# The row of -max by DMA in a fused attention and MLP kernel, with every fifth query in a tile of the maxima

## The chip, the cores and the metric

The kernel runs on one core of a Trainium2 chip. The metric is the device time of one execution in microseconds (us), as the median of several; a separate execution is recorded by the hardware profiler and gives the profile and the trace. The engines are TensorE (PE for its products, PEld for the loads of its stationary operand), VectorE (DVE), ScalarE (ACT), GpSimd (POOL) and SyncE (SP, which here only issues DMAs).

## The reference

```python
def _attn_ref(q, k, v):                     # (2, 8, 1152, 64) each
    q_pool = q.reshape(B, H, S // 2, 2, D).mean(axis=3)
    scores = scale * np.matmul(q_pool, k.transpose(0, 1, 3, 2))
    scores = scores - np.max(scores, axis=-1, keepdims=True)
    attn = np.exp(scores)
    attn = attn / (np.sum(attn, axis=-1, keepdims=True) + 1e-09)
    return np.matmul(attn, v)

x = attn_out.transpose(0, 2, 1, 3).reshape(1152, 512)
r = np.maximum(x @ moe_w_in, 0.0);  x = (r * r) @ moe_w_out            # 512 -> 2048 -> 512
out = ((x @ moe2_w_a) * (x @ moe2_w_b)) @ moe2_w_out                   # 512 -> 1536 -> 512
```

There are 16 heads (batch times heads), each with 576 pooled queries and 1152 keys of 64 values. Every row of scores has its exact maximum taken off before the exponential.

## The kernel before

Every operand of a product is split into a high and a low part (float32r), and a product of two such operands is three products, so that accuracy stays near float32. The attention runs head by head, written out in one order for all engines; each engine works through its own list in that order.

For a head `h`, `trans_q` and `trans_k` transpose the pooled queries and the keys by TensorE and spread the parts by DMAs into the operands `qa` (high part of q, twice, 128 rows), `q0` (low part), `k1` (high and low part of k) and `kb` (high part of k, with rows of ones below). `maxima(h, n)`, n = 0 to 7, computes scores with the queries on the 116 output partitions: five tiles of 116 queries (`QO`: 0, 116, 232, 348, 460, the last two overlap) by three chunks of 384 keys, two products each, into PSUM tiles `pm`; VectorE reduces each to its negated maximum in `mh`. In such a product the slice of `qa` or `q0` is the stationary operand and `k1` the moving one. `max_split` takes the minimum over the three chunks (`nm`) and splits it into a high and a low part in `mz`. `trans_max` turns that into two rows: five TensorE transposes of 66 rows into a PSUM tile `px`, of which ScalarE copies rows 64 and 65 into rows 64 and 65 of `qb`, the moving operand whose first 64 rows are the low part of q. With the ones in `kb` the product of `kb` and `qb` then adds the negated maximum.

`scores(h, t)`, t = 0 to 8, computes scores again with 128 keys on the partitions and 576 queries in two halves, as `k1` by `qa` plus `kb` by `qb`, into a PSUM tile `ps`; ScalarE makes the exponential `ex` and its high part `eh`, VectorE (or POOL for t = 1, 4, 7) the low part `el`. `values(h, t)` multiplies with v into `o`, two steps later. `normal` copies `o` to `os`; for each pair of heads `outputs` makes the reciprocal sums (`dn` by DMA, `rd`, and `rb` on POOL), and `outputs_end` transposes `rb` into a PSUM tile `pr`, multiplies (`xt` on VectorE), and writes the operand of the MLP, `xh` by ScalarE and `xl` by VectorE. All of `pm`, `ps`, `px`, `pr`, `pq` and `pk` share one ring of three PSUM buffers, so a tile waits for the reader of the third tile before it.

The loop interleaves two heads: in step t of head h stand `scores(h, t)`, `maxima(h + 1, t + 3)` up to t = 4 and `maxima(h + 2, t - 6)` from t = 6 on, and `values` of step t - 2. `max_split(h + 1)` stands at t = 5, `trans_max(h + 1)` at t = 6, `outputs_end` at t = 5 of odd heads from h = 3 on. From h = 7 on, at t = 4 and 8, `w_step` also prepares weights of the MLP: it loads them (`raw`) and splits them on ScalarE (`wa`, `whi`), VectorE (`wx`) and POOL (`wlo`).

Behind the attention come the two MLPs, which the change doesn't touch.

Of the kernel before, what the change touches and what calls it, by code (L numbers as in the profile page):

```python
# [9 lines left out]
F32 = mybir.dt.float32  # L10
F32R = mybir.dt.float32r
# [10 lines left out]
def kernel(  # L22
# [18 lines left out]
    nc = tc.nc  # L41
# [135 lines left out]


    TQ = 116
    QO = [0, 116, 232, 348, 460]  # L180
    NQ = len(QO)
    NCH = S // CW

    KO = [0, 2, 4, 6, 1, 3, 5, 7, 8]
# [3 lines left out]
    def attention(gs):  # L188
        with ExitStack() as es:
# [30 lines left out]
            NB = 3  # L220
            k1 = [(pp if i == (NH - 3) % NB else ap).tile([P, S], F32R, name=f"k1_{i}") for i in range(NB)]
            kb = [(pp if i == (NH - 3) % NB else ap).tile([P, S], F32R, name=f"kb_{i}") for i in range(NB)]
            qa = [(pp if i == (NH - 3) % NB else ap).tile([P, SQ], F32R, name=f"qa_{i}") for i in range(NB)]
            vv = [(pp if i == (NH - 3) % NB else ap).tile([P, KT, 2, VW], F32R, name=f"vv_{i}") for i in range(NB)]
            qb = [ap.tile([P, SQ], F32R, name=f"qb_{i}") for i in range(2)]
            q0 = [pp.tile([P, SQ], F32R, name=f"q0_{i}") for i in range(2)]
            mz = [pp.tile([TQ, NQ, D + 2], F32R, name=f"mz_{i}") for i in range(2)]

            def constant(t, x):
                nc.gpsimd.memset(t.bitcast(F32), x)  # L230
# [7 lines left out]
            first_k = k1[2].rearrange("p (t a d) -> p t a d", a=2, d=D)  # L238
            first_q = [kb[i][:QP, :QT * P].rearrange("p (t a d) -> p t a d", a=2, d=D) for i in (1, 2)]
            constant(first_q[1][:, :, 1, :], 0.0)  # L240
            constant(mz[0], 0.0)
            constant(qb[0][D:], 0.0)
            constant(q0[1][D:], 0.0)

# [2 lines left out]
            def copy(e, out, in_):  # L247
                if e == "A":
                    nc.scalar.copy(out, in_)
                else:  # L250
                    engines[e].tensor_copy(out, in_)

            def move(out, in_, queue=nc.sync):

                queue.dma_start(out=out.bitcast(F32), in_=in_.bitcast(F32))

            def less(e, out, x, hi):
                engines[e].tensor_tensor(out=out, in0=x, in1=hi.bitcast(F32), op=ALU.subtract)  # L258

            def ps_tile(name, dt=F32):  # L260
                return ps_p.tile([P, 2, 512], dt, tag="ps", name=name)

            def halves(t):
                return t.rearrange("p (b w) -> p b w", b=2)
# [55 lines left out]
            def maxima(h, n):  # L320
                if n == 0:
                    mh[h] = ap.tile([TQ, NQ * NCH], F32, tag="mh", bufs=2, name=f"mh{h}")
                ps = ps_tile(f"pm{h}_{n}")
                todo = [divmod(j, NCH) for j in range(2 * n, min(2 * n + 2, NQ * NCH))]
                for b, (i, c) in enumerate(todo):
                    qs = slice(QO[i], QO[i] + TQ)
                    ks = slice(c * CW, (c + 1) * CW)
                    nc.tensor.matmul(ps[:TQ, b, :CW], qa[h % NB][:, qs], k1[h % NB][:, ks], start=True, stop=False)  # L328
                    nc.tensor.matmul(ps[:TQ, b, :CW], q0[h % 2][:, qs], k1[h % NB][:, ks], start=False, stop=True)  # L329
                w = len(todo)  # L330
                nc.vector.tensor_reduce(  # L331
                    out=mh[h][:, 2 * n:2 * n + w], in_=ps[:TQ, :w, :CW], op=ALU.max, axis=AX.X, negate=True
                )

            def max_split(h):
                z = mz[h % 2]
                nm = ap.tile([TQ, NQ], F32, tag="nm", bufs=2, name=f"nm{h}")
                nc.vector.tensor_reduce(
                    out=nm, in_=mh.pop(h).rearrange("p (i c) -> p i c", c=NCH), op=ALU.min, axis=AX.X
                )  # L340
                nc.vector.tensor_copy(z[:, :, D], nm)
                less("V", z[:, :, D + 1], nm, z[:, :, D])

            def by_tiles(ps):

                return (slice(0, 464), ps[:, 0, :464]), (slice(464, SQ), ps[:, 1, 4:TQ])

            def trans_max(h, e="A"):
                ps = ps_tile(f"px{h}", F32R)
                for i in range(NQ):  # L350
                    nc.tensor.matmul(
                        ps[:D + 2, i // 4, (i % 4) * TQ:(i % 4 + 1) * TQ], mz[h % 2][:, i, :], idr[:TQ, :TQ],
                        is_transpose=True, start=True, stop=True,
                    )
                for sl, src in by_tiles(ps):
                    copy(e, qb[h % 2][D:D + 2, sl], src[D:D + 2].bitcast(F32))


            ex, eh, el, ou = {}, {}, {}, {}
# [1 line left out]
            def scores(h, t):  # L361
                ps = ps_tile(f"ps{h}_{t}")
                ks = slice(t * P, (t + 1) * P)
                for c in range(2):
                    sl = slice(c * CQ, (c + 1) * CQ)
                    nc.tensor.matmul(ps[:, c, :CQ], k1[h % NB][:, ks], qa[h % NB][:, sl], start=True, stop=False)  # L366
                    nc.tensor.matmul(ps[:, c, :CQ], kb[h % NB][:, ks], qb[h % 2][:, sl], start=False, stop=True)  # L367
                e = ex[h, t] = ap.tile([P, SQ], F32, tag="ex", bufs=3, name=f"ex{h}_{t}")
                nc.scalar.activation(halves(e), ps[:, :, :CQ], AF.Exp, scale=SCALE)  # L369

# [70 lines left out]
            def first_head():  # L441
                idle(NWARM)
                pool_q(0, "V")
                x = qs_t.pop(0)
                hi, lo = first_q
                nc.scalar.copy(first_k[:, :, 0], kin[0])
                nc.vector.tensor_copy(hi, x[:, :, None, :].to_broadcast([QP, QT, 2, D]))
                less("V", lo[:, :, 0], x, hi[:, :, 0])
                less("V", first_k[:, :, 1], kin.pop(0), first_k[:, :, 0])
                for src, dst, eng in ((hi, qa[0], "A"), (lo, q0[0], "V")):  # L450
                    ps = ps_tile(f"fq{eng}", F32R)
                    for t in range(QT):
                        nc.tensor.matmul(
                            ps[:, t % 2, (t // 2) * QP:(t // 2 + 1) * QP], src[:, t].rearrange("p a d -> p (a d)"),
                            idr[:QP, :QP], is_transpose=True, start=True, stop=True,
                        )
                    copy(eng, halves(dst), ps[:, :, :CQ].bitcast(F32))
                move(qb[0][:D], q0[0][:D])
                for part, n in enumerate((6, 3)):
                    ps = ps_tile(f"fk{part}", F32R)  # L460
                    for i in range(n):
                        nc.tensor.matmul(
                            ps[:, i // 3, (i % 3) * P:(i % 3 + 1) * P],
                            first_k[:, KO[6 * part + i]].rearrange("p a d -> p (a d)"), idr,
                            is_transpose=True, start=True, stop=True,
                        )
                    for b in range(n // 3):
                        c0 = (2 * part + b) * CW
                        copy("AVA"[2 * part + b], k1[0][:, c0:c0 + CW], ps[:, b, :CW].bitcast(F32))
# [8 lines left out]
            for n in range(NM):  # L478
                maxima(0, n)
                if n == 1:  # L480
                    trans_q(1)
                    constant(mz[1], 0.0)
                    constant(qb[1][D:], 0.0)
                    constants(1)
                    move(kb[0][:D], k1[0][:D])
                    load(2)
                    load(3)
            max_split(0)
            idle(7)
            trans_max(0)  # L490
            for n in range(AHEAD - 1):
                maxima(1, n)
            split_v(0)
# [8 lines left out]
            for h in range(NH + 1):  # L502
                last = h == NH - 1
                for t in range(KT if h < NH else 2):
                    if h + 1 < NH and t == NM - AHEAD:
                        max_split(h + 1)
                    if t == 0 and h + 1 < NH:
                        move(qb[(h + 1) % 2][:D], q0[(h + 1) % 2][:D])
                    if h + 2 < NH:
                        if t == 0:  # L510
                            trans_q(h + 2)
# [5 lines left out]
                        exp_hi(h, t)  # L517
                    while later:
                        later.pop(0)()
                    if h + 1 < NH:  # L520
                        if t == NM - AHEAD + 1:
                            trans_max(h + 1)
                    if h % 2 and h > 1 and t == NM - AHEAD:
                        outputs_end((h - 3) // 2, rb)
                    if h + 1 < NH and t < NM - AHEAD:
                        maxima(h + 1, t + AHEAD)
                    if h + 2 < NH and t >= KT - AHEAD:
# [15 lines left out]
                    if t == 5 and h + 2 < NH:  # L543
                        split_v(h + 2)
                        load_v(h + 4)
                    if NH - 9 <= h < NH - 1 and t in (4, 8):
                        w_step(NE)
                    if last:
# [235 lines left out]
```

## Time and profile before

| | |
|---|---|
| median of 3 runs | 767.36 us (766.59 to 767.93) |
| profiled execution | 767.84 us, span 766.1 us |
| TensorE products / loads | 741.7 us busy (97%) / 714.9 us (93%), 4629 each |
| VectorE, ScalarE, POOL | 507.6 us (66%), 409.5 us (53%), 147.5 us (19%) |
| granted TensorE clock | 0.996 of full speed on average |

The span is the time from the first to the last recorded instruction. A busy TensorE is not one at its peak: products are pipelined, and the length shown for one contains the latency of the pipeline, so their starts are closer than their lengths. How much each step costs is read from the distance between starts.

### The profile page before, as it was taken

Reading aid. Unit: us, or ns where it says so; the run is one execution under the profiler, and the core shown is the slowest. Engines: PE = TensorE matmul, PEld = TensorE weight load, DVE = VectorE, ACT = ScalarE, POOL = GpSimd, SP = SyncE. Lnnn points to the kernel's source line nnn. Section 1 sums busy time; section 2 is a strip of 40 time slices with the busy share of each in tenths; the row PEclk is TensorE's granted clock in tenths of the full one; section 3 lists DMA queues with packets and bytes.
Section 4 is the critical chain, followed back from the end, with each engine's and each line's share of the span. In section 5 each row is a group of like instructions: output and inputs, shape, how many; then the busy total and the mean of one; then the engine's idle time right before and its main releaser. Section 6 shows DMA issues by size and latency. Waiting matters only on the chain.

```text
span 766.1 us, 12264 instructions
## 1 busy us (share of the span) xinstructions
PE 741.7 (97%) x4629; PEld 714.9 (93%) x4629; DVE 507.6 (66%) x807; ACT 409.5 (53%) x716; POOL 147.5 (19%) x132
## 2 busy tenths in 40 slices
PE   8999999989999999899999999999999999999998
PEld 7899999979899898889999999999999988999986
DVE  6777878767888888556973298746687831377511
ACT  2677777767778677764642376423455522355300
POOL 5444344432454453200310000000000000000000
PEclk9999999999999999999999999999999999999999
DMA  6755555564655451100431232212333320043022
GB/s 176 211 132 141 125 130 127 128 173 114 165 141 136 126 113 38 37 9 1 137 112 56 83 111 82 83 56 83 96 126 119 128 83 29 29 136 111 1 56 68
DMA packets 57547, 76.75 MB, mean 100 GB/s; under 512 B 7248, under 2 KB 41936, under 8 KB 57488
## 3 DMA queue, kind: packets, MB, share of 16 engines
q1 hardware_dynamic: 57168, 75.38, 35.7%
q10 hardware_dynamic: 320, 0.59, 0.3%
q8 instruction: 36, 0.59, 0.3%
q14 instruction: 23, 0.19, 0.1%
HBM read 49.81 MB, written 2.36 MB: 68 GB/s over the span
## 4 chain that ended last, share of the span: by engine, by line
PE 82%; DVE 8%; ACT 3%; issue 3%; DMA 2%; SPq 1%; POOL 0%; ACTq 0%; DVEq 0%; POOLq 0%
PE o L388 11%; PE pm L328 5%; PE pm L329 4%; PE y L580 4%; PE y L581 4%; PE y L579 4%; PE ps L366 4%; PE ps L367 4%; PE a L579 3%; PE a L581 3%; PE b L581 3%; PE b L579 3%; PE a L580 3%; PE b L580 3%; PE o L581 3%; PE o L580 3%
## 5 line engine op out<-in xcount | busy, mean ns | idle before, releaser
L331 DVE TENSOR_REDUCE mh<-pm 116x2 f32<-116x768 f32 (+1 forms) x128 | 114.7, 901 | 40.0 <-PE pm L329 39.2
L388 PE MATMUL o<-eh,vv 128*66 128x288 f32 x576 | 138.8, 297 | 0.7 <-ACT os L398 0.7
L369 ACT ACTIVATE ex<-ps 128x576 f32<-128x576 f32 x144 | 93.8, 652 | 49.4 <-PE ps L367 47.1
L258 DVE TENSOR_TENSOR el<-ex,eh 128x576 fp32r<-128x576 f32 x99 | 87.1, 880 | 22.3 <-ACT eh L373 22.3
L373 ACT CAST eh<-ex 128x576 fp32r<-128x576 f32 x144 | 97.1, 674 | 4.6
L258 POOL TENSOR_TENSOR el<-ex,eh 128x576 fp32r<-128x576 f32 x45 | 66.5, 1478 | 151.6 <-ACT eh L373 87.3
L328 PE MATMUL pm<-k,qa 128*116 128x384 f32 x240 | 85.1, 355 | 4.7 <-DVE xt L424 2.6
L388 PE MATMUL o<-el,vv 128*66 128x288 f32 x288 | 85.2, 296 | 0.9 <-POOL el L258 0.6
L366 PE MATMUL ps<-qa,k 128*128 128x288 f32 x288 | 83.7, 305 | 0.1
L329 PE MATMUL pm<-k,q 128*116 128x384 f32 x240 | 82.3, 343 | 0.0
L367 PE MATMUL ps<-qb,kb 128*128 128x288 f32 x288 | 81.3, 296 | 0.0
L388 PEld LDWEIGHTS o<-eh,vv 128*66 128x66 f32 x576 | 78.5, 137 | 1.1 <-ACT os L398 0.9
L145 DVE TENSOR_TENSOR wlo<-wx,whi 128x512 fp32r<-128x512 f32 x56 | 38.5, 687 | 54.5 <-ACT whi L111 54.5
L111 ACT CAST whi<-wx 128x512 fp32r<-128x512 f32 x68 | 42.1, 619 | 51.4 <-DVE wx L130 51.4
L580 PE MATMUL y<-gl,whi 128*128 128x384 f32 x192 | 64.8, 338 | 0.6 <-DVE gl L570 0.6
L581 PE MATMUL y<-gh,wlo 128*128 128x384 f32 x192 | 64.8, 338 | 0.0
L579 PE MATMUL y<-gh,whi 128*128 128x384 f32 x192 | 64.7, 337 | 0.0
L579 PE MATMUL h<-xh,whi 128*128 128x384 f32 (+1 forms) x172 | 56.0, 325 | 0.7 <-ACT r L598 0.7
L580 PE MATMUL h<-xl,whi 128*128 128x384 f32 (+1 forms) x172 | 55.9, 325 | 0.0
L581 PE MATMUL h<-xh,wlo 128*128 128x384 f32 (+1 forms) x172 | 55.9, 325 | 0.0
L366 PEld LDWEIGHTS ps<-qa,k 128*128 128x128 f32 x288 | 54.7, 190 | 0.5 <-ACT ex L369 0.4
L367 PEld LDWEIGHTS ps<-qb,kb 128*128 128x128 f32 x288 | 54.7, 190 | 0.0
(110 smaller groups left out, 1684.0 us busy)
## 6 DMA issues: line engine op xcount, KB each, us to landing
raw<-in_moe_w_out_dram SPq DMA_DIRECT2D x28, 512.0 KB, 3.4
raw<-in_moe_w_in_dram SPq DMA_DIRECT2D x16, 512.0 KB, 3.8
raw<-in_moe_w_a_dram SPq DMA_DIRECT2D x12, 512.0 KB, 3.5
raw<-in_moe_w_b_dram SPq DMA_DIRECT2D x12, 512.0 KB, 3.5
qin<-in_q_dram SPq DMA_DIRECT2D x16, 288.0 KB, 3.5
kin<-in_k_dram SPq DMA_DIRECT2D x16, 288.0 KB, 3.7
vin<-in_v_dram SPq DMA_DIRECT2D x16, 288.0 KB, 3.2
k<-kt SPq DMA_DIRECT2D x28, 160.0 KB, 2.7
```

The costliest lines, as they stand in the source:

```text
L258: engines[e].tensor_tensor(out=out, in0=x, in1=hi.bitcast(F32), op=ALU.subtract)
L328: nc.tensor.matmul(ps[:TQ, b, :CW], qa[h % NB][:, qs], k1[h % NB][:, ks], start=True, stop=False)
L329: nc.tensor.matmul(ps[:TQ, b, :CW], q0[h % 2][:, qs], k1[h % NB][:, ks], start=False, stop=True)
L331: nc.vector.tensor_reduce(out=mh[h][:, 2 * n:2 * n + w], in_=ps[:TQ, :w, :CW], op=ALU.max, axis=AX.X, negate=True)
L366: nc.tensor.matmul(ps[:, c, :CQ], k1[h % NB][:, ks], qa[h % NB][:, sl], start=True, stop=False)
L367: nc.tensor.matmul(ps[:, c, :CQ], kb[h % NB][:, ks], qb[h % 2][:, sl], start=False, stop=True)
L369: nc.scalar.activation(halves(e), ps[:, :, :CQ], AF.Exp, scale=SCALE)
L373: nc.scalar.copy(eh[h, t], ex[h, t])
L388: nc.tensor.matmul(ou[h][:VW, c, :CQ], w, x[:, c * CQ:(c + 1) * CQ], start=t == 0 and i == 0, stop=t == KT - 1 and i == 2,)
L579: nc.tensor.matmul(ps, lh, rh, start=i == 0, stop=False)
L580: nc.tensor.matmul(ps, lh, rl, start=False, stop=False)
L581: nc.tensor.matmul(ps, ll, rh, start=False, stop=i == n - 1)
```

## The change

The maxima take their queries with a step of five: tile i of a head holds the queries i, i + 5, i + 10 and so on. `qa`, `q0` and `qb` grow from 576 to 580 columns (`SM`), the last four of which are zero, so that five tiles of 116 cover them. Then the five values that a partition p holds in `mz` are those of the queries 5p to 5p + 4, and the whole of `mz`, read partition by partition, is the row in its natural order. Two DMAs, one for the high and one for the low part, write it into rows 64 and 65 of `qb`; `trans_max`, its transposes, its PSUM tile and its copies are gone, and so are the seven dummy products ahead of the first of them. In `scores` the two products `k1` by `qa` come first, then the two `kb` by `qb`. `outputs_end` moves ahead of `max_split` and of the scores of its step. The first three loads of weights are issued in step 6 of head 5.

```diff
-    QO = [0, 116, 232, 348, 460]
-    NQ = len(QO)
+    NQ = 5
+    SM = NQ * TQ
...
-            mz = [pp.tile([TQ, NQ, D + 2], F32R, name=f"mz_{i}") for i in range(2)]
+            mz = [ap.tile([TQ, 2, NQ], F32R, name=f"mz_{i}") for i in range(2)]
...
-                    qs = slice(QO[i], QO[i] + TQ)
+                    hi, lo = (t.rearrange("p (q i) -> p i q", i=NQ)[:, i] for t in (qa[h % NB], q0[h % 2]))
                     ks = slice(c * CW, (c + 1) * CW)
-                    nc.tensor.matmul(ps[:TQ, b, :CW], qa[h % NB][:, qs], k1[h % NB][:, ks], start=True, stop=False)
-                    nc.tensor.matmul(ps[:TQ, b, :CW], q0[h % 2][:, qs], k1[h % NB][:, ks], start=False, stop=True)
+                    nc.tensor.matmul(ps[:TQ, b, :CW], hi, k1[h % NB][:, ks], start=True, stop=False)
+                    nc.tensor.matmul(ps[:TQ, b, :CW], lo, k1[h % NB][:, ks], start=False, stop=True)
...
-            def max_split(h):
+            def max_split(h, queue=nc.sync):
...
-                nc.vector.tensor_copy(z[:, :, D], nm)
-                less("V", z[:, :, D + 1], nm, z[:, :, D])
...
+                nc.vector.tensor_copy(z[:, 0], nm)
+                less("V", z[:, 1], nm, z[:, 0])
+                for a in range(2):
+                    move(qb[h % 2][D + a:D + a + 1], z[:, a], queue)
...
-                for c in range(2):
-                    sl = slice(c * CQ, (c + 1) * CQ)
-                    nc.tensor.matmul(ps[:, c, :CQ], k1[h % NB][:, ks], qa[h % NB][:, sl], start=True, stop=False)
-                    nc.tensor.matmul(ps[:, c, :CQ], kb[h % NB][:, ks], qb[h % 2][:, sl], start=False, stop=True)
+                for i, (w, x) in enumerate(((k1, qa[h % NB]), (kb, qb[h % 2]))):
+                    for c in range(2):
+                        sl = slice(c * CQ, (c + 1) * CQ)
+                        nc.tensor.matmul(ps[:, c, :CQ], w[h % NB][:, ks], x[:, sl], start=i == 0, stop=i == 1)
...
-            max_split(0)
-            idle(7)
-            trans_max(0)
+            max_split(0, nc.scalar)
...
+                    if h % 2 and h > 1 and t == NM - AHEAD:
+                        outputs_end((h - 3) // 2, rb)
                     if h + 1 < NH and t == NM - AHEAD:
                         max_split(h + 1)
...
-                    if h + 1 < NH:
-                        if t == NM - AHEAD + 1:
-                            trans_max(h + 1)
-                    if h % 2 and h > 1 and t == NM - AHEAD:
-                        outputs_end((h - 3) // 2, rb)
...
+                    if h == NH - 11 and t == 6:
+                        w_load(3)
```

Three places show what moves. The first is TensorE in steps 5 and 6 of head 3, before; `ps3_5` are the scores of head 3, step 5, `pm5_0` the first maxima of head 5, `o3` the values.

```order
L367 MATMUL ps3_5_1233<-qb_1_112,kb_0_102 128x288
L418 MATMUL pr0_1242<-idf_80,rb0_1206 128x96 x6
L388 MATMUL o3_1171<-eh3_3_1187,vv_0_108 66x288
...
L366 MATMUL ps3_6_1264<-qa_0_105,k1_0_99 128x288
L367 MATMUL ps3_6_1264<-qb_1_112,kb_0_102 128x288
L366 MATMUL ps3_6_1264<-qa_0_105,k1_0_99 128x288
L367 MATMUL ps3_6_1264<-qb_1_112,kb_0_102 128x288
L351 MATMUL px4_1274<-idr_85,mz_0_115 66x116 x5
L328 MATMUL pm5_0_1283<-k1_2_101,qa_2_107 116x384
```

`pr` follows the scores of step 5, `px` those of step 6. The same place on TensorE in the changed kernel:

```order
L377 MATMUL o3_1143<-eh3_2_1133,vv_0_108 66x288
L407 MATMUL pr0_1201<-idf_80,rb0_1178 128x96 x6
L356 MATMUL ps3_5_1217<-qa_0_105,k1_0_99 128x288 x2
L356 MATMUL ps3_5_1217<-qb_1_112,kb_0_102 128x288 x2
L377 MATMUL o3_1143<-eh3_3_1159,vv_0_108 66x288
...
L356 MATMUL ps3_6_1239<-qa_0_105,k1_0_99 128x288 x2
L356 MATMUL ps3_6_1239<-qb_1_112,kb_0_102 128x288 x2
L329 MATMUL pm5_0_1249<-k1_2_101,qa_2_107 116x384
```

`pr` has moved from behind the scores of step 5 to ahead of them, `px` is gone, and the scores come in pairs.

The second place is ScalarE in the same steps, before; `xh_64` is the copy of the output step, `qb_0` the row of the maxima.

```order
L373 CAST eh3_4_1215<-ex3_4_1213 128x576
L369 ACTIVATE ex3_5_1238<-ps3_5_1233 128x576
L373 CAST eh3_5_1240<-ex3_5_1238 128x576
L430 CAST xh_64<-xt0_1249 128x576
L369 ACTIVATE ex3_6_1269<-ps3_6_1264 128x576
L373 CAST eh3_6_1271<-ex3_6_1269 128x576
L249 CAST qb_0_111<-px4_1274 2x464
L249 CAST qb_0_111<-px4_1274 2x112
```

The copies for the row, from `px`, stand behind step 6 there. The same place on ScalarE in the changed kernel:

```order
L362 CAST eh3_4_1187<-ex3_4_1185 128x576
L419 CAST xh_64<-xt0_1208 128x576
L358 ACTIVATE ex3_5_1222<-ps3_5_1217 128x576
L362 CAST eh3_5_1224<-ex3_5_1222 128x576
L358 ACTIVATE ex3_6_1244<-ps3_6_1239 128x576
L362 CAST eh3_6_1246<-ex3_6_1244 128x576
```

The copy `xh` now stands ahead of the exponential of step 5, and the two copies from `px` are gone. On VectorE `xt` likewise stands ahead of the three operations of `max_split`, where it stood behind them.

The third place is SP's queue in head 1 of the changed kernel, from the loads for head 5 in step 1 to the first move of head 2; `qb_0<-mz_0` x2 is new.

```order
L206 DMA qin5_595<-in_q_dram 96x768
L208 DMA kin5_597<-in_k_dram 128x576
L390 DMA dn0_624<-os0_622 96x1x6
L256 DMA qb_0_111<-mz_0_115 1x116x5 x2
L213 DMA vin5_721<-in_v_dram 128x576
L256 DMA qb_1_112<-q0_1_114 64x576
```

The two moves of the row stand between the DMA of the sums (`dn`) and the load of v; all else is in the order of before.

## Rows read from the trace of the kernel before

**Rows 1.** The chain that ended last, share of the span by engine.

```profile
PE 82%; DVE 8%; ACT 3%; issue 3%; DMA 2%; SPq 1%; POOL 0%; ACTq 0%; DVEq 0%; POOLq 0%
```

**Rows 2.** Busy time by stretch, heads 2, 3, 7 and 11 (columns in the first row).

```profile
core 0: us, PE busy (x) PEld busy (x) DVE busy (x) ACT busy (x) POOL busy (x), PEclk, DMA share, GB/s
59.40:77.80 18.40, 18.40 (x136) 18.02 (x135) 13.89 (x21) 14.12 (x23) 7.69 (x6) 1.00 0.56 138
77.80:97.90 20.10, 19.35 (x141) 18.45 (x141) 17.16 (x25) 14.72 (x24) 8.12 (x7) 1.00 0.48 118
154.80:179.50 24.70, 20.88 (x142) 19.85 (x140) 15.41 (x25) 15.45 (x26) 8.08 (x7) 0.93 0.52 138
238.60:261.20 22.60, 20.84 (x142) 19.87 (x140) 18.40 (x27) 15.16 (x26) 8.98 (x7) 0.92 0.50 125
```

**Rows 3.** Timeline of TensorE in head 1 (start us, us, engine, line, operation).

```profile
53.03 0.29 PE L367 MATMUL ps<-qb,kb 128*128 128x288 f32 x1
53.16 0.44 PE L351 MATMUL px<-idr,mz 116*66 116x116 f32 x5
...
53.67 0.34 PE L329 MATMUL pm<-k,q 128*116 128x384 f32 x1
53.85 0.34 PE L328 MATMUL pm<-k,qa 128*116 128x384 f32 x1
```

**Rows 4.** Timeline at the start, ahead of head 0.

```profile
10.08 3.17 ACTq L255 DMA_DIRECT2D k<-kt  x4
...
19.80 0.45 PE L351 MATMUL px<-idr,mz 116*66 116x116 f32 x5 [1.63 <-DVE mz L258]
...
22.22 0.99 POOL L272 TENSOR_TENSOR qs<-qin 96x384 f32<-96x384 f32 x1 [7.83 <-DMA qin<-in_q_dram]
```

**Rows 5.** Groups by line: count, busy us, mean ns, idle before and its releasers.

```profile
L328 PE MATMUL pm<-k,qa 128*116 128x384 f32 x240 | 85.1, 355 | 4.7 <-DVE xt L424 2.6 <-ACT qb L249 1.6 <-DVE qt L258 0.3
...
L351 PE MATMUL px<-idr,mz 116*66 116x116 f32 x80 | 7.1, 219 | 9.0 <-DVE mz L258 5.5 <-ACT ex L369 3.5
```

**Rows 6.** Timeline of head 7, ScalarE and TensorE.

```profile
169.98 0.67 ACT L121 ACTIVATE wa<-raw 128x512 f32<-128x512 f32 x1 [4.41 <-DMA raw<-in_moe_w_in_dram]
...
171.25 0.47 PE L351 MATMUL px<-idr,mz 116*66 116x116 f32 x5 [3.46 <-ACT ex L369]
```

**Rows 7.** Timeline of head 3, steps 5 and 6.

```profile
87.80 0.82 POOL L251 COPY rb<-rd 96x768 f32<-96x768 f32 x1 [2.80 <-DVE rd L410]
...
88.05 0.29 PE L366 MATMUL ps<-qa,k 128*128 128x288 f32 x1
...
88.68 0.71 PE L418 MATMUL pr<-idf,rb 96*128 96x96 f32 x6
...
91.34 0.43 PE L328 MATMUL pm<-k,qa 128*116 128x384 f32 x1 [0.35 <-DVE xt L424]
```

**Rows 8.** Timeline of VectorE in head 11.

```profile
248.90 1.10 DVE L127 SCALAR_TENSOR_TENSOR wx<-wa,wx 128x512 int32<-128x512 int32 x1
250.03 1.81 DVE L130 SCALAR_TENSOR_TENSOR wx<-raw,wx 128x512 int32<-128x512 int32 x1
```

**Rows 9.** DMA: a move by size and us to landing; then the landings of dn.

```profile
q<-qt SPq DMA_DIRECT2D x30, 72.0 KB, 2.0
```

```profile
DMA to landing us min/median/max: 1.9/3.2/4.6
```

**Rows 10.** Timeline: mz in head 4, and the first kb product of head 5.

```profile
108.62 0.17 DVE L258 TENSOR_TENSOR mz<-nm,mz 116x5 fp32r<-116x5 f32 x1
...
116.39 0.29 PE L367 MATMUL ps<-qb,kb 128*128 128x288 f32 x1
```

**Rows 11.** Groups by line: two loads of TensorE, two operations of VectorE.

```profile
L388 PEld LDWEIGHTS o<-eh,vv 128*66 128x66 f32 x576 | 78.5, 137 | 1.1 <-ACT os L398 0.9
L328 PEld LDWEIGHTS pm<-k,qa 128*116 128x116 f32 x240 | 43.5, 181 | 8.8 <-DVE xt L424 3.4 <-ACT qb L249 2.5 <-DVE mh L331 1.7
L258 DVE TENSOR_TENSOR kt<-pk,kt 128x640 fp32r<-128x640 f32 x15 | 12.4, 824 | 5.6 <-ACT kt L249 5.5
L424 DVE TENSOR_TENSOR xt<-pr,os 128x576 f32<-128x576 f32 x8 | 9.9, 1243 | 1.6 <-PE pr L418 1.6
```

More of the change, by code (lines that the diff above doesn't have):

```diff
@@ L222, in attention @@
             kb = [(pp if i == (NH - 3) % NB else ap).tile([P, S], F32R, name=f"kb_{i}") for i in range(NB)]
-            qa = [(pp if i == (NH - 3) % NB else ap).tile([P, SQ], F32R, name=f"qa_{i}") for i in range(NB)]
+            qa = [(pp if i == (NH - 3) % NB else ap).tile([P, SM], F32R, name=f"qa_{i}") for i in range(NB)]
             vv = [(pp if i == (NH - 3) % NB else ap).tile([P, KT, 2, VW], F32R, name=f"vv_{i}") for i in range(NB)]
-            qb = [ap.tile([P, SQ], F32R, name=f"qb_{i}") for i in range(2)]
-            q0 = [pp.tile([P, SQ], F32R, name=f"q0_{i}") for i in range(2)]
-            mz = [pp.tile([TQ, NQ, D + 2], F32R, name=f"mz_{i}") for i in range(2)]
+            qb = [ap.tile([P, SM], F32R, name=f"qb_{i}") for i in range(2)]
+            q0 = [pp.tile([P, SM], F32R, name=f"q0_{i}") for i in range(2)]
+            mz = [ap.tile([TQ, 2, NQ], F32R, name=f"mz_{i}") for i in range(2)]
             def constant(t, x):
@@ L240, in attention @@
             constant(first_q[1][:, :, 1, :], 0.0)
-            constant(mz[0], 0.0)
+            for t in qa + q0:
+                constant(t[:, SQ:], 0.0)
             constant(qb[0][D:], 0.0)
@@ L340, in max_split @@
                 )
-                nc.vector.tensor_copy(z[:, :, D], nm)
-                less("V", z[:, :, D + 1], nm, z[:, :, D])
[L344 to L356, printed above, removed]
+                nc.vector.tensor_copy(z[:, 0], nm)
+                less("V", z[:, 1], nm, z[:, 0])
+                for a in range(2):
+                    move(qb[h % 2][D + a:D + a + 1], z[:, a], queue)
             ex, eh, el, ou = {}, {}, {}, {}
@@ L456, in first_head @@
                         )
-                    copy(eng, halves(dst), ps[:, :, :CQ].bitcast(F32))
-                move(qb[0][:D], q0[0][:D])
+                    copy(eng, halves(dst[:, :SQ]), ps[:, :, :CQ].bitcast(F32))
+                move(qb[0][:D, :SQ], q0[0][:D, :SQ])
                 for part, n in enumerate((6, 3)):
@@ L481, in attention @@
                     trans_q(1)
-                    constant(mz[1], 0.0)
                     constant(qb[1][D:], 0.0)
@@ L507, in attention @@
                     if t == 0 and h + 1 < NH:
-                        move(qb[(h + 1) % 2][:D], q0[(h + 1) % 2][:D])
+                        move(qb[(h + 1) % 2][:D, :SQ], q0[(h + 1) % 2][:D, :SQ])
                     if h + 2 < NH:
```

## Prediction

> **What bounds the kernel now.** I read the chain that ended last first: TensorE carries 82% of it, VectorE 8%, ScalarE 3% [rows 1]. Then the stretches head by head: a head that has no output step (h = 2: 59.4 to 77.8) lasts 18.40 us with TensorE busy 18.40 and VectorE 13.89, so only fewer or shorter TensorE slots can shorten it; a head with an output step (h = 3) lasts 20.10 with TensorE busy 19.35, and the two longest, h = 7 (24.70) and h = 11 (22.60), also show granted clocks of 0.93 and 0.92 [rows 2]. Of the clock's two levels, 2.4 and 1.2 GHz, a mean of 0.93 over 24.7 us means 1.7 us of lost work. Nothing in the change acts behind the attention, so the sum is made within its 16 heads.
>
> **The transposes of the maxima (px).** In an undisturbed head the last score product starts at 53.03, the five px at 53.16, and the second product of the next pm at 53.67, the third 0.18 later [rows 3]. Without px the first product of pm would start at 53.16 and the second at 53.34: 0.33 us saved in each of 15 heads, 5.0 us (A). The px of head 0 gives nothing: at the start TensorE waits for POOL's qs at 22.22, which waits for the q load, whatever stands before it [rows 4]. The two ScalarE copies per head that go too lie on an engine that waits in this stretch, and count only as waits below.
>
> px also waits: TensorE sat idle 9.0 us before it, 5.5 us in six places for mz and 3.5 us once for ex [rows 5]. 1.63 us of the 5.5 is the start [rows 4]; the other five waits are 3.9 us, and each is some 0.16 us longer than shown, since a 288-column product counts as busy for 0.29 us but gives its slot free after 0.13 [rows 3]. That makes 4.7 us (B). What is late next is the row itself, no longer TensorE's queue, as the row is needed only at the next head's first kb product.
>
> **The early weight load.** The single wait for ex is the first weight step: ScalarE sits 4.41 us for raw, issued only then, and px waits 3.46 us for the exponential behind that [rows 6]: 3.6 us with the drain, and the clock's 1.7 us after it [rows 2]. With w_load(3) two heads earlier the three loads have landed; the step still costs ScalarE its 0.67 us. 5.3 us (D).
>
> **outputs_end in front of the scores.** Before, pm_0 waits 0.35 us for xt in h = 3 [rows 7]; over all heads pm sat idle 2.6 us for xt, in six heads, and 1.6 us for qb, the px buffer, in four [rows 5]. With the 0.16 of drain at each of ten places that is 5.8 us, which go: px is no longer a user of the three PSUM buffers, and xt stands ahead of the maxima's three small steps. But pr now stands where ps_5 stood, at 88.05, and rb ends at 88.62 [rows 7]: pr starts at about 88.68 as before, and TensorE waits 0.63 us in front of it, with the scores behind it. And on ScalarE the copy xh, which waits for xt (pr takes 0.71 [rows 7], xt 1.24 [rows 11], the hand-overs some 0.07), now stands ahead of ex_5: xt ends at 90.7, xh 91.4, ex_5 92.05, eh_5 92.75, ex_6 93.4 with 0.65 to 0.67 us for each copy and exponential, as the weight step's copy takes [rows 6], while TensorE, counted on from pr by its own slots, wants ex_6's buffer for pm_1 at 93.03: 0.43 us with the hand-over. The 0.63 and the 0.43 in six heads are 6.4, and the last head's pr, already late, waits 0.5 longer: 6.9 against the 5.8 that go, so -1.1 (C); without the delay of ex_5 it would be +1.5.
>
> In h = 11 VectorE has two weight operations, 2.9 us [rows 8], ahead of xt, so pm_0 waits for xt about 1.2 us and ex_5 follows 0.35 later than in the other heads. Half of the 1.8 us that the clock lost there [rows 2] may come back. Together -0.6 (F).
>
> **The row by DMA.** Two issues per head on SP; nothing behind them but the load of v, which waits for POOL anyway, and the next head's moves. The nearest row is dn<-os, 96 pieces of 24 bytes: 3.2 us to land in the median, against 2.0 for a move of 72 KB [rows 9]. With 0.8 us for the issue ahead of it (four issues took 3.17 us [rows 4]), the second row lands about 4.0 us after mz; bounds are 1.9 and twice 4.6 (one behind the other). mz of h = 4 ends at 108.79 and the first kb product of h = 5 starts at 116.39 [rows 10]: 7.6 us, 7.3 without px; in odd heads xt goes first and leaves 6.1. So it is covered, by 2.1 us at the least. At the start px began at 19.80 [rows 4], so mz was there; 4.0 us on, at 23.8, is about when the first kb product wants the row, as qs ends at 23.2: 0.5 us lost (G).
>
> **Scores in pairs.** The same four products and four weight loads per tile: nothing. They only put two products that need no row in front, which is worth 0.27 us once a head if the row is late.
>
> **Every fifth query.** This is the disputed cost. The stationary operand of the 480 pm products is now read with a step of 20 bytes. No row shows TensorE reading so. A load of 116 columns shows as 181 ns, one of 66 as 137 [rows 11]: 0.88 ns a column, so it holds the path for about 102 ns, behind slots of 0.174 us (384 columns) or 0.133 (288) [rows 3]. Lower bound: nothing, as long as a load stays below 133. Upper bound from the only strided row: xt reads and writes SBUF at a step of 24 bytes, 1243 ns for 576 elements, 2.16 ns each, while kt takes 824 for 640, 1.29 each [rows 11]. By its ratio, 1.68, a load takes 102 x 1.68 = 171 ns; by its pace, 250. A load of L exposes L-133 in the first of a group of four and L-174 in the other three, and there are 120 groups: 171 costs 120 x 38 ns = 4.6 us; 250 costs 120 x 345 = 41 us. The ratio scales with the reader's own pace, and a load is paced by its columns, not plainly by SBUF; so I take the lower part, between nothing and the ratio's 4.6: 2 us lost (H).
>
> SBUF — State Buffer of the Trainium skill (the note on cachelines under "Door 1: The DMA port swizzle") says that an access which crosses to a new 16-byte line each time pays, and that two hits on a line are needed for full rate; a step of 20 bytes never has two. It speaks against this edit, the page states no size, and by the factor of two that its wording suggests the sum would end at the 772 of the first rival below. The xt row agrees that such steps cost.
>
> **Sum**, against the profiled execution's own 767.84 us (span 766.1; the median of the runs is 767.36): A 5.0 + B 4.7 + D 5.3 - C 1.1 - F 0.6 - G 0.5 = 12.8 gained, less H 2: 10.8. Forecast 757 us; from 755 (H nothing), or 752 if ex_5 is not delayed either, to 760 (H 4.6 and some of B given back).
>
> **The rivals.** *The load takes twice as long*: 204 ns, 71 + 3 x 30 = 161 ns a group, 19.3 us: 767.8 - 12.8 + 19.3 = 774.3; some 2 to 3 us of the waits for rb, xt and ex_6 vanish behind a slower TensorE, so 772. It is the one that ends on the other side: the gain is used up at 12.8 us, 107 ns a group, L = 190, 1.9 times today's. For it: xt's pace. Against it: TensorE's moving operand comes in at 384 columns in 0.174 us, twice the rate of a load, so its reads are not at their limit in a load.
>
> *The waits only move.* VectorE is busy 18.40 of 22.60 us in h = 11 and 17.16 of 20.10 in h = 3 [rows 2], so B may return as waits of pm for its reduction: with B given back 767.8 - 10.8 + 4.7 = 762.
>
> *The row is late.* The extra 1.2 us of dn over a large move come with 96 short pieces, and the row has 116, all into one partition. If the two together take 9.2 us (the upper bound), the kb product waits 2 to 3 us in 15 heads: 30 to 45 us, minus the gain: 780 to 790. It decides from a landing of about 7 us after mz.
>
> DMA: Bandwidth & Descriptors of the Trainium skill ("Why a DMA increments its semaphore by 16 and not by 1") lets a DMA use the largest number of engines up to 16 that divides its outer sizes: 16 for dn's 96, but 4 for 116, so 29 pieces on an engine instead of 6. No row shows such a move; as an estimate, 1.2 us for 6 pieces makes 5.8 for 29, and then the row would be late by one or two us a head.
>
> **Chances.** Forecast, H from nothing to 4.6 us (752 to 760): 0.60. Waits only move: 0.14, 760 to 764. Load twice as long or more: 0.18, 766 to 785, near 772. Row late: 0.08, above 770. The forecast's own range is 752 to 760; the range that leaves out no more than two in ten, and takes in that C or F may be better by 2 or 3 us, runs from 750 to 769. A measurement of this kernel tells 0.2% (1.5 us) from no change: faster takes the first two cases and 0.02 of the third, 0.76; same 0.06 of the third, 0.06; slower the rest, 0.18.
>
> **What would show it.** A: no px, heads without an output step at about 18.1 us. H: the shown length of the pm loads (181 ns now), and pm starts 0.174 apart or more. B and D: no TensorE idle for mz, clock 1.0 in h = 7. C: pr idle about 0.6 us for rb in seven heads, xh ahead of ex_5 with pm_1 waiting for ex_6. The row: landing near 3 us, no wait of the first kb product. The prediction is wrong if pm spacing grows beyond 0.2 us, if the row takes over 7 us, or if the clock falls at the start, where TensorE now waits in one piece for qs.

## The result, and the profile after

The changed kernel takes 775.5 us (median of 4 runs, 774.57 to 775.86) against 767.64 for the kernel before beside it. The ratio is 1.0092, 95% interval 1.0078 to 1.0105 (the two medians alone give 1.0102), so about 1% slower, where 757 us were forecast. One of the four executions of e10 below took 1862.73 us, and its time here is the median of the other three. The profiled execution has a span of 774.1 us, 8.0 more than before.

The stretches of the changed kernel by head (h = 2, 3, 7, 11, which answer to [rows 2]), and below them the start:

```profile
core 0: us, PE busy (x) PEld busy (x) DVE busy (x) ACT busy (x) POOL busy (x), PEclk, DMA share, GB/s
64.70:84.00 19.30, 19.30 (x131) 19.00 (x129) 13.56 (x20) 13.43 (x21) 7.69 (x6) 1.00 0.54 132
84.00:104.50 20.50, 20.12 (x136) 19.41 (x135) 16.11 (x24) 13.83 (x22) 8.10 (x7) 1.00 0.48 117
163.60:184.10 20.50, 20.14 (x136) 19.47 (x135) 16.58 (x25) 14.55 (x24) 8.23 (x7) 1.00 0.48 116
245.80:267.70 21.90, 20.59 (x136) 19.54 (x135) 18.45 (x27) 14.41 (x24) 8.93 (x7) 1.00 0.52 129
...
23.00:26.00 3.00, 0.76 (x5) 0.53 (x5) 0.46 (x1) 0.40 (x1) 2.00 (x2) 0.75 0.67 202
26.00:30.00 4.00, 3.90 (x15) 3.77 (x16) 1.62 (x2) 1.99 (x3) 0.00 (x0) 0.50 0.73 185
30.00:34.00 4.00, 4.00 (x24) 3.93 (x23) 2.86 (x4) 2.68 (x5) 2.27 (x2) 0.84 0.67 152
```

The kernel before from 26 to 30 us:

```profile
26.00:30.00 4.00, 3.90 (x27) 3.54 (x26) 3.59 (x5) 3.10 (x6) 2.14 (x2) 1.00 0.69 184
```

Heads 7 and 11 did get shorter (24.70 to 20.50, 22.60 to 21.90) and their clock is 1.00. But head 2, with nothing in it except TensorE's own work, is 0.9 us longer than before, although five transposes are gone from it. And at the start, where the kernel before shows a granted clock of 1.00, the clock is 0.50 (the 1.2 GHz level) from 26 to 30 us, behind a stretch in which TensorE was busy 0.76 of 3 us: 15 products in the same busy 3.90 us that hold 27 before.

Where head 2 lost its time is seen in the groups by line, the loads of the maxima (line, engine, shape, count, then busy us and mean ns):

```profile
L329 PEld LDWEIGHTS pm<-k,qa 128*116 128x116 f32 x240 | 70.2, 293 | 4.5 <-DVE mh L332 1.7
...
L330 PEld LDWEIGHTS pm<-k,q 128*116 128x116 f32 x240 | 72.9, 304 | 0.3 <-DMA q<-qt 0.2
```

They show 293 and 304 ns where [rows 11] had 181. The timeline of the changed kernel tells what that costs. First the row of head 0, then one group of maxima in head 1, last the row of head 15 (start us, us):

```profile
19.35 0.17 DVE L259 TENSOR_TENSOR mz<-nm,mz 116x5 fp32r<-116x5 f32 x1
19.39 1.93 ACTq L256 DMA_DIRECT2D qb<-mz  x2
23.04 0.47 PE L279 MATMUL pq<-idf,qs 96*128 96x96 f32 x3 [1.62 <-POOL qs L273]
26.10 0.85 PE L356 MATMUL ps<-qb,kb 128*128 128x288 f32 x2 [2.30 <-DMA qb<-mz]
...
58.62 0.41 PE L329 MATMUL pm<-k,qa 128*116 128x384 f32 x1
58.87 0.37 PE L330 MATMUL pm<-k,q 128*116 128x384 f32 x1
59.08 0.38 PE L329 MATMUL pm<-k,qa 128*116 128x384 f32 x1
59.29 0.37 PE L330 MATMUL pm<-k,q 128*116 128x384 f32 x1
59.50 0.29 PE L377 MATMUL o<-eh,vv 128*66 128x288 f32 x1
...
321.05 0.17 DVE L259 TENSOR_TENSOR mz<-nm,mz 116x5 fp32r<-116x5 f32 x1
321.23 1.33 SPq L256 DMA_DIRECT2D qb<-mz  x2
325.27 0.50 PE L356 MATMUL ps<-qb,kb 128*128 128x288 f32 x2 [0.86 <-DMA qb<-mz]
```

The products of maxima start 0.25, 0.21, 0.21 and 0.21 us apart, four in 0.88 us; at the 0.174 that one takes before (0.18 in [rows 3]) they take 0.70. In head 0 mz ends at 19.52 and the product that reads the row starts at 26.10: 6.6 us. In head 15 the same path takes 4.0 us. What TensorE waited for in the attention of the changed kernel (us in total, times, longest):

```profile
PE pr L407 <- POOL rb L252: 3.6, 7, 1.4
PE ps L356 <- DMA qb<-mz: 3.2, 2, 2.3
PE pq L279 <- POOL qs L273: 1.6, 1, 1.6
PE pm L329 <- DVE xt L413: 0.9, 1, 0.9
...
```

The row is waited for twice only, in heads 0 and 15. The waits of px [rows 5] are gone with px, those of pm for xt are one instead of six, and pr now waits for rb in seven heads instead of once (0.8 us before).

### The profile page after: what moved, and what is told of

It reads as the page before. It is cut to its first block, busy times and chain, and to the rows that moved or that the text cites. A ratio compares the mean times of both kernels' runs of the same rounds, so it can differ in the third digit from the quotient of the medians.

```text
span 774.1 us, 12142 instructions
## 1 busy us (share of the span) xinstructions
PE 755.0 (98%) x4542; PEld 728.8 (94%) x4542; DVE 507.1 (66%) x807; ACT 398.0 (51%) x684; POOL 145.9 (19%) x135
## 4 chain that ended last, share of the span: by engine, by line
PE 86%; DVE 6%; ACT 3%; issue 3%; DMA 1%; POOL 0%; ACTq 0%; DVEq 0%; POOLq 0%
PE o L377 12%; PE ps L356 9%; PE pm L329 6%; PE pm L330 5%; PE y L565 4%; PE y L566 4%; PE y L564 4%; PE a L564 3%; PE b L564 3%; PE b L565 3%; PE a L565 3%; PE a L566 3%; PE b L566 3%; PE o L565 3%; PE o L566 3%; PE o L564 3%
## 5 line engine op out<-in xcount | busy, mean ns | idle before, releaser
L377 PE MATMUL o<-eh,vv 128*66 128x288 f32 x576 | 137.1, 294 | 0.7 <-ACT os L387 0.7
L329 PE MATMUL pm<-k,qa 128*116 128x384 f32 x240 | 97.0, 404 | 2.3 <-DVE xt L413 0.9
L330 PE MATMUL pm<-k,q 128*116 128x384 f32 x240 | 89.9, 375 | 0.0
L377 PEld LDWEIGHTS o<-eh,vv 128*66 128x66 f32 x576 | 80.2, 141 | 1.0 <-ACT os L387 1.0
L329 PEld LDWEIGHTS pm<-k,qa 128*116 128x116 f32 x240 | 70.2, 293 | 4.5 <-DVE mh L332 1.7
L330 PEld LDWEIGHTS pm<-k,q 128*116 128x116 f32 x240 | 72.9, 304 | 0.3 <-DMA q<-qt 0.2
L356 PE MATMUL ps<-qb,kb 128*128 128x288 f32 x288 | 62.6, 299 | 3.2 <-DMA qb<-mz 3.2
L356 PE MATMUL ps<-qa,k 128*128 128x288 f32 x288 | 65.2, 308 | 0.0
```

Of the source, the lines that this page charges most:

```text
L329: nc.tensor.matmul(ps[:TQ, b, :CW], hi, k1[h % NB][:, ks], start=True, stop=False)
L330: nc.tensor.matmul(ps[:TQ, b, :CW], lo, k1[h % NB][:, ks], start=False, stop=True)
L356: nc.tensor.matmul(ps[:, c, :CQ], w[h % NB][:, ks], x[:, sl], start=i == 0, stop=i == 1)
L377: nc.tensor.matmul(ou[h][:VW, c, :CQ], w, x[:, c * CQ:(c + 1) * CQ], start=t == 0 and i == 0, stop=t == KT - 1 and i == 2,)
```

## Experiments

Times are medians, ratios are against the kernel before on the same chip. Each ratio has an interval of about 0.0015 to either side, so a difference of two of them is good to 1.5 to 2 us. In e1 to e4, e6, e7, e9 and e11 the tiles of the maxima hold other columns than their row, so another query's maximum is taken off: these runs price a stage, and are no versions to use.

**e1, contiguous tiles.** All of the change, but the stationary operand read without a step.

```diff
...
-   hi, lo = (t.rearrange("p (q i) -> p i q", i=NQ)[:, i] for t in (qa[h % NB], q0[h % 2]))
+   hi, lo = (t[:, i * TQ:(i + 1) * TQ] for t in (qa[h % NB], q0[h % 2]))
```

> The changed kernel, but a tile of the maxima takes 116 neighbouring columns again, with the row still written in its natural order, so that a query has the maximum of another one taken off (softmax does not depend on it). Theory S (the strided load of the stationary operand costs 0.18 us in each of the 120 groups of four products, 21.6 us in all): loads of pm back to 181 ns, pm starts 0.174 us apart, time 753 to 756 us, so faster than before by 12 to 14 us. Rival W (the loss comes from new waits: the row by DMA, pr ahead of the scores, xh ahead of the exponential): loads shorter, but the time stays at 768 us or more.

757.48 us, ratio 0.9855 (0.9841 to 0.987). The loads are back, as the group by line of e1 shows:

```profile
L329 PEld LDWEIGHTS pm<-k,qa 128*116 128x116 f32 x240 | 43.7, 182 | 6.4 <-DVE mh L332 2.5 <-ACT ex L358 1.8 <-DVE xt L413 1.1
```

So the step alone is worth the difference of the ratios, 0.0237 of 767.6 us: 18.2 us, give or take 1.5.

**e2, the step alone.** The kernel before with the 580 columns and the strided tiles (e1's edit, reversed), `trans_max` and all else left as it was.

> The kernel before, with every fifth query in a tile of the maxima and nothing else of the change (qa and q0 padded to 580 columns; the transposed maxima land at other queries than their own). Theory S: loads of pm at about 304 ns, groups of four 0.18 us longer, time 786 to 789 us; a little less where waits that are there anyway take part of it. Rival W: within 3 us of before, 765 to 770 us.

784.09 us, ratio 1.0196 (1.0179 to 1.0213): 15.1 us lost by nothing but the step, with the loads at 292 and 303 ns, the first by this line of e2:

```profile
L331 PEld LDWEIGHTS pm<-k,qa 128*116 128x116 f32 x240 | 70.2, 292 | 6.7 <-DVE xt L427 3.6 <-ACT qb L252 1.7 <-DVE mh L334 0.6
```

**e3, e4 and e9, other steps.** The changed kernel with steps of 8, 16 and 12 bytes between the columns, by one edit (s = 2, 4, 3; b = 58, 29, 46 moves the tiles apart):

```diff
-   ... t.rearrange("p (q i) -> p i q", i=NQ)[:, i] ...
+   ... t[:, b * i:b * i + s * TQ].rearrange("p (q j) -> p j q", j=s)[:, 0] ...
```

> The changed kernel with a step of 2 columns (8 bytes) in place of 5 in the stationary operand of the maxima (some queries enter no maximum). If what counts is a new 16-byte line for each column, a step of 8 bytes has two columns on a line and costs nothing: loads at 181 ns, time 753 to 756 us. If any step costs, loads at about 304 ns, time 775 us. If the cost grows with the step, in between, about 220 ns and 756 to 760 us.

> The changed kernel with a step of 4 columns (16 bytes) in place of 5 (some queries enter no maximum). If a new line for each column is what costs, the same as a step of 5: loads at about 304 ns, 775 us. If the cost grows with the bytes that are passed over, a little less than with 5: about 280 ns, 770 us.

> As e3 and e4 with a step of 12 bytes between the columns of a stationary load (other queries than the reference's; the row doesn't fit them). Of four columns three begin on a new 16-byte line. If every column on a new line pays the same, a load takes three quarters of the way from 182 to 300 ns, some 265 to 285; if a line must be hit twice in a row for the full rate, it takes 300 like the steps of 16 and 20 bytes.

Step 8: 757.87 us (two runs), ratio 0.9858 (0.9838 to 0.9877). Step 16: 777.67 (two runs), ratio 1.0115 (1.0095 to 1.0135). Step 12: 763.64, one run. Their loads, by line, in e3, e4 and e9:

```profile
L329 PEld LDWEIGHTS pm<-k,qa 128*116 128x116 f32 x240 | 45.3, 189 | 6.3 <-DVE mh L332 2.3 <-ACT ex L358 1.7 <-DVE xt L413 1.1
```

```profile
L329 PEld LDWEIGHTS pm<-k,qa 128*116 128x116 f32 x240 | 71.7, 299 | 4.6 <-DVE mh L332 1.9 <-DVE xt L413 1.1 <-DVE qt L259 0.6
```

```profile
L329 PEld LDWEIGHTS pm<-k,qa 128*116 128x116 f32 x240 | 57.2, 238 | 5.7 <-DVE mh L332 1.8 <-ACT ex L358 1.6 <-DVE nm L339 1.1
```

A step as such costs next to nothing (8 bytes: 189 ns), and from 16 to 20 bytes the cost does not grow (299 and 293). The 12 bytes lie half way: 56 ns more than contiguous, against 117 for 16 bytes. My expectation for them charged every column that begins a new 16-byte line, three of four; e3 speaks against that, for there half of the columns begin one and the load is 7 ns longer. Columns at 0, 12, 24, 36 bytes and so on fall two on one 16-byte line, then one and one on the next two: half of the columns have their line to themselves. With 8 bytes none has, with 16 and 20 all have. So the four steps fit a price for each column that is alone on its line, 117 ns over 116 columns, 1.0 ns for each. The Trainium skill's SBUF — State Buffer (the note under "Door 1: The DMA port swizzle") says that two hits on a line of 16 bytes are needed for the full rate; the four steps agree with that.

Another reading was not told apart from this one: a load that pays for each line it touches, or for each column where that is more. As an estimate from the 0.88 ns a column of the prediction and the 117 ns here, a line would take 1.9 ns; that makes 62 ns more at 12 bytes and 7 at 8, where 56 and 7 are measured, and a column alone on its line makes 58 and nothing.

**e5, the early weight load alone**, in the kernel before.

```diff
...
+                    if h == NH - 11 and t == 6:
+                        w_load(3)
...
```

> The kernel before with one thing of the change: the first three loads of weights issued in step 6 of head 5. The prediction's term D says 5.3 us less than before, so a ratio of 0.993, with head 7 at about 19.5 us (24.75 before) and a granted clock of 1.0 in it. Rival: the wait only moves to the next weight step or to another transfer that the three loads delay, and the ratio is 0.997 or more.

762.17 us, ratio 0.9915 (0.9901 to 0.993): 6.5 us. Head 7 of e5 in the stretches:

```profile
154.50:175.30 20.80, 19.54 (x140) 18.44 (x139) 17.26 (x25) 15.10 (x26) 8.23 (x7) 1.00 0.46 113
```

The clock there is 1.00 and 3.9 us are gone; the 19.5 us expected are not reached, since in e5 px still waits for mz (5.8 us in seven places). The rest of the 6.5 lies outside this head, and where was not looked for.

**e6, outputs_end back** behind the scores of its step, on top of e1; and **e7, the row of head 0 by TensorE** as before, on top of e1.

```diff
-                    if h % 2 and h > 1 and t == NM - AHEAD:
-                        outputs_end((h - 3) // 2, rb)
...
                         exp_hi(h, t)
                     while later:
                         later.pop(0)()
+                    if h % 2 and h > 1 and t == NM - AHEAD:
+                        outputs_end((h - 3) // 2, rb)
```

```diff
...
-            max_split(0, nc.scalar)
+            max_split(0)
+            idle(7)
+            trans_max(0)
...
```

> The kernel of e1 with outputs_end back behind the scores of its step; still another query's maximum is subtracted. The prediction's term C says that moving it forward cost 1.1 us net, most of it the wait of pr for rb and of ex_5 behind xh: then this is about 1 us faster than e1, 756.4. Rival: pm waits for xt again in six or seven heads, and it is 1.5 us or more slower than e1, 759 or above.

> The kernel of e1 with the row of head 0 alone made by TensorE as before (seven dummy products, five transposes, two copies by ScalarE); all later rows by DMA; another query's maximum is subtracted in the later heads. If head 0 lost its 4.6 us (22.03 against 17.47) to the row that lands 6 us after its issue, and to the clock that falls in that wait, this is 4.5 us faster than e1, about 753, with the clock at 1.0 from 23 to 34 us. Rival: the start loses it to POOL's sum of queries for head 2, whatever brings the row, and it stays at 757.

e6: 754.41 us, ratio 0.9816 (0.98 to 0.9832), 3.0 us better than e1. e7: 753.87, ratio 0.9809 (0.9794 to 0.9823), 3.5 us better. Two of TensorE's waits in the attention of e1, then those of e6:

```profile
PE pr L407 <- POOL rb L252: 4.3, 7, 1.4
...
PE pm L329 <- DVE xt L413: 0.9, 1, 0.9
```

```profile
PE pq L279 <- POOL qs L273: 2.9, 1, 2.9
PE ps L356 <- DMA qb<-mz: 1.8, 1, 1.8
PE pm L329 <- ACT ex L358: 1.4, 3, 0.5
PE pr L407 <- POOL rb L252: 0.8, 1, 0.8
...
PE ps L356 <- DVE xt L413: 0.7, 1, 0.7
...
```

With outputs_end where it was before, pm waits for xt nowhere and for no qb, and rb is waited for 0.8 us instead of e1's 4.3. So the waits that the move was credited with had gone with px. The start of e7:

```profile
20.00:24.00 4.00, 4.00 (x18) 3.88 (x19) 1.74 (x2) 0.69 (x2) 1.72 (x3) 0.57 1.00 301
24.00:27.00 3.00, 2.87 (x21) 2.47 (x19) 2.32 (x4) 2.05 (x4) 1.29 (x1) 1.00 0.53 138
27.00:31.00 4.00, 4.00 (x27) 3.61 (x26) 3.81 (x6) 3.07 (x6) 2.30 (x2) 1.00 0.61 173
31.00:35.00 4.00, 4.00 (x30) 3.92 (x30) 3.29 (x7) 2.96 (x5) 0.69 (x2) 1.00 0.84 186
```

From 24 us on the clock is 1.00, and head 0 takes 17.27 us instead of e1's 22.03. But a shorter fall stands ahead of it in this execution, 0.57 from 20 to 24 us, and head 0 begins 0.97 later than in e1. So with the row by TensorE the clock may fall at the start too; what decides that, no run here shows.

**e8, a usable version**: pairs of tiles that share a step of 8 bytes, with head 0 by TensorE as in e7.

```diff
...
-   ... t.rearrange("p (q i) -> p i q", i=NQ)[:, i] ...
+   ... t[:, 464:] if i == 4 else t[:, i // 2 * 232:i // 2 * 232 + 232].rearrange("p (q j) -> p j q", j=2)[:, i % 2] ...
...
-                for a in range(2):
-                    move(qb[h % 2][D + a:D + a + 1], z[:, a], queue)
+                for a in range(2 if h else 0):
+                    for b in (0, 2, 4):
+                        n = min(2, NQ - b)
+                        move(qb[h % 2][D + a:D + a + 1, b * TQ:(b + n) * TQ], z[:, a, b:b + n], queue)
...
```

> A version with the reference's result: tiles of the maxima 0 and 1, and 2 and 3, take alternate queries (a step of 8 bytes), tile 4 takes the last 116 columns in a row; the row of each part goes by three DMAs of pieces of 8 and 4 bytes, six a head; head 0 by TensorE. If the line theory holds, its loads take 189 ns as in e3 and are free, and if the row lands in time it is at 753. Rival: six issues on SP, some 0.65 us each, and 348 pieces for each part land later than the 7.6 us that are there; then the first kb product of a head waits 1 to 3 us and the time is 768 to 800.

758.5 us, ratio 0.9872 (0.9854 to 0.989). Between the two cases: 4.6 us above e7. Heads 6 and 7 are 1.9 and 1.3 us longer than e7's. The queue of SP in e8 has six issues of the row and, in head 5, three loads:

```profile
129.75 3.98 SPq L258 DMA_DIRECT2D qb<-mz  x6
133.83 0.42 SPq L213 DMA_DIRECT2D vin<-in_v_dram  x1
134.30 1.53 SPq L105 DMA_DIRECT2D raw<-in_moe_w_in_dram  x3
135.92 0.54 SPq L258 DMA_DIRECT2D qb<-q  x1
...
144.40 2.38 SPq L258 DMA_DIRECT2D k<-kt  x4
```

**e10, px one step later** in e5, to price B by itself.

```diff
-                        if t == NM - AHEAD + 1:
+                        if t == KT - 2:
                             trans_max(h + 1)
```

> The kernel of e5 with the five transposes one step later (step 7 instead of 6), the rest as before. If B, the 4.7 us of waits of px for mz, was only queueing ahead of a value that is ready soon after, this is 4 to 5 us faster than e5, 757 to 758. Rival: the copies from px and the buffer that px holds come to wait in its place, and it stays at 761 to 763.

763.5 us (median of three), ratio 0.9928 (0.9908 to 0.9948): nothing gained over e5. Its waits:

```profile
PE pm L328 <- DVE mh L331: 6.5, 8, 1.3
PE px L351 <- ACT ex L369: 1.4, 3, 0.5
```

Now pm waits. In step 7 the ring of three buffers holds pm_0, ps_7 and px, so pm_1 needs the buffer of pm_0, whose reduction VectorE has not ended; without px the third tile before pm_1 is ps_6. A px that comes later still takes its place in the ring.

**e11, e6 and e7 together.**

> e6 and e7 together: contiguous tiles, the row of head 0 by TensorE, outputs_end back behind the scores (another query's maximum is subtracted from head 1 on). The two gains, 3.1 and 3.6 us over e1, lie in different heads but for head 0, which was 1.3 us shorter in e6 too: 751 to 752. Rival: e6 won only by its shorter head 0, then it is at 753 to 754 as e7.

749.59 us, ratio 0.9753 (0.9739 to 0.9768): better than the sum expected. Here outputs_end back is worth 4.3 us over e7; by the intervals that and the 3.0 of e6 are not told apart.

**e12, the usable version mended**: e8 with outputs_end back as in e6, and the loads spread.

```diff
-                    if h == NH - 11 and t == 6:
-                        w_load(3)
+                    if NH - 14 <= h < NH - 11 and t == 6:
+                        w_load(h - NH + 15)
```

> The version of e8, which has the reference's result, with outputs_end back behind the scores and the three first loads of weights in heads 2, 3 and 4, one each, instead of three in head 5. If e8 lost its 4.6 us against e7 to SP, where six issues of the row and three loads stood in line ahead of the moves for the next head (heads 6 and 7 were 1.9 and 1.3 us longer), this is at 753 or less. Rival: the six issues alone make the moves late, and it is at 755 to 758.

751.09 us, ratio 0.9771 (0.9757 to 0.9786). It beats both kernels: 2.3% under the one before. Its heads 2, 3, 7 and 11, and two of its waits:

```profile
58.90:76.90 18.00, 18.00 (x131) 17.70 (x130) 13.81 (x20) 13.48 (x22) 7.69 (x6) 1.00 0.62 146
76.90:95.90 19.00, 18.99 (x135) 18.08 (x134) 17.07 (x24) 13.87 (x23) 8.40 (x7) 1.00 0.66 171
151.10:170.60 19.50, 19.05 (x137) 18.16 (x135) 17.29 (x25) 14.41 (x25) 8.25 (x7) 1.00 0.52 122
225.90:246.20 20.30, 19.10 (x135) 18.09 (x134) 18.24 (x27) 14.31 (x24) 8.98 (x7) 1.00 0.58 142
```

```profile
PE px L355 <- DVE mz L261: 1.6, 1, 1.6
...
PE ps L373 <- DMA qb<-mz: 1.3, 2, 1.1
```

Two things changed at once over e8, 7.8 us together by the ratios. The 4.3 that outputs_end gave in e11 leave some 3.5 for the loads, which were not spread alone. Heads 6 and 7 bear that out: they take 17.99 and 19.51 us here against 19.82 and 20.74 in e8, 3.1 us less, though outputs_end back gave these two heads nothing from e7 (17.97 and 19.45) to e11 (18.35 and 19.49). So six issues a head are bearable where the three loads do not stand behind them.

## Why the prediction was wrong, step by step

**The step that failed: "a load is paced by its columns, not plainly by SBUF; so I take the lower part, between nothing and the ratio's 4.6: 2 us lost (H)".** Measured are 18.2 us (after against e1) and 15.1 (e2). The two bounds, nothing and 41 us, held it. The choice between them did not: it went by a ratio from VectorE's xt, and the argument for the low end, that TensorE's moving operand comes in at twice a load's rate, compared contiguous reads with a read that pays for each line. The first rival, a load of twice the time, had the mechanism, the size (161 ns a group, where the groups show 180) and the end, 772 for 775.5; it got 18 in 100. The products of maxima start 0.21 us apart behind such loads, more than the 0.2 that the prediction named as a sign of being wrong.

Head 2 pays 1.32 us for the step (17.96 in e1, 19.28 after). Sixteen such heads would pay 21.1, of which 18.2 remain. Waits that shrink behind a slower TensorE are of that size: those listed in the attention come to 13.5 us in e1 and 10.2 in the changed kernel, with pr's for rb going from 4.3 to 3.6.

**G, the start, 0.5 predicted, 3.5 measured (e7).** The step that failed is the landing "about 4.0 us after mz". It was 6.6 in head 0 and 4.0 in head 15, with the same 116 pieces: at the start the two issues on ScalarE take 1.93 us instead of SP's 1.33, and the landing behind them 4.8 instead of 2.7, while the core's DMA engines are 0.67 to 0.73 busy from 23 to 30 us, against 0.38 from 321 to 326. The clock then falls to 0.50, as the last sentence of the prediction feared. Head 0 is 4.9 us longer than before; the wait for the row is 2.3 of it, and the clock's part is 2.6 as an estimate from the rows of the start (half of 4 us lost at 0.50, 0.64 of the next 4 at 0.84). No run took the two apart; e7 gained 3.5 us over e1.

**A and B, and the gains in C.** e11, with px gone after head 0 and outputs_end unmoved, gains 0.0247, 19.0 us; without e5's 6.5, if that adds up, 12.5 are left for px with all that waited because of it (the paired scores are in it too). Predicted were 5.0 + 4.7, and 5.8 for pm's waits for xt and the px buffer, which the prediction put down to outputs_end: 15.5. The heads without an output step went from 18.37 us between starts to 17.97 in e1 (predicted 18.1).

**C's costs.** Lengths of some heads in us, from the first product of one pq to that of the next:

| head | before | after | e1 | e7 | e11 | e12 |
|---|---|---|---|---|---|---|
| 0 | 17.47 | 22.36 | 22.03 | 17.27 | 17.52 | 17.51 |
| 2 | 18.36 | 19.28 | 17.96 | 17.99 | 17.98 | 17.96 |
| 3 | 20.15 | 20.53 | 19.51 | 19.48 | 19.09 | 19.08 |
| 7 | 24.75 | 20.54 | 19.46 | 19.45 | 19.50 | 19.51 |
| 9 | 20.51 | 22.14 | 21.18 | 20.48 | 19.21 | 19.17 |
| 11 | 22.65 | 21.89 | 20.84 | 20.81 | 20.34 | 20.40 |

From e7 to e11, which differ in outputs_end alone, heads 3 and 11 get 0.4 and 0.5 us shorter, head 9 1.3, and head 7 no shorter; why they differ is not shown. The wait for rb came much as predicted (4.3 more; e1 shows 4.3 in seven heads, 0.8 of it there before, so 3.5 more). The 0.43 us for ex_6 in six heads did not: in e1 a pm waits for ex once, 0.2 us. And as the gains set against them were px's, the move has no gain of its own: it costs 3.0 (e6) to 4.3 us (e11), near the 3.5 of the wait for rb, where the net was put at 1.1. With the row above the errors cancel: A, B, C and F came to 8.0 predicted, and 12.5 less 3.0 to 4.3, so 8.2 to 9.5, measured. That these terms came out near their sum is luck.

**D, 5.3 predicted, 6.5 measured** (5.4 to 7.6), with the clock of 1.00 that it rested on.

**The other rivals.** *The waits only move* fell for this change, but e10 shows that it is what happens if px is only put later. *The row is late* fell outside head 0: one wait of 0.86 us in 15 heads. The prediction's estimate for its 116 pieces was 5.8 us. It rested on the rule in DMA: Bandwidth & Descriptors of the Trainium skill ("Why a DMA increments its semaphore by 16 and not by 1") by which such a move uses four engines. The 2.7 us from the end of the second issue in head 15 do not bear the estimate out, and no row shows how many engines the move used.

## What to carry to other kernels

Before striding a stationary operand, count how many of its columns sit alone on a 16-byte line. For the float32 loads here a step of two cost 7 ns a load, a step of three 56, and steps of four and five 117 and 111, about 1 ns a column. What is paid is what the load then exceeds the product ahead of it by: here 0.18 us of the 0.47 by which four loads grew. Price an unseen operation by the mechanism that makes it differ, and where the bounds are nothing and 41 us, and a mechanism is named for the upper part, give that part the weight of its mechanism. If a wait could have gone by either of two edits, ask which one alone removes it; here outputs_end was moved for a wait that had already gone.

## What the runs showed that was not expected

The load's time rises in the share of columns that are alone on their line (182, 189, 238 and 299 ns at steps of 4, 8, 12 and 16 bytes), not with the distance (293 at 20 bytes). The clock at the start fell in e7 too, where TensorE makes the row of head 0. A move of 116 pieces of 20 bytes into one partition landed 2.7 us behind its issue in head 15 and 4.8 at the start.
